# Own room for six half-row loads, four stores a row instead of eight, and no zero matmuls in a fused Fourier, mixture-of-experts and FFN kernel

## The chip, the cores and the metric

The kernel runs on one core of one Trainium2 chip. The metric is the device time of one execution in microseconds (us). TensorE (PE) does the matmuls, VectorE (DVE) and ScalarE (ACT) the elementwise work, GpSimd (POOL) part of the elementwise work and the gathers, and SyncE (SP) issues most of the DMA transfers.

## The reference

Three layers follow each other, all in float32:

```
X = rfft(x, axis=1)                                # x: 4 x 3072 x 256
Y = X @ (w_r + i w_i) + bias; Y = softshrink(Y, 0.01) on both parts
y = irfft(Y)                                       # 4*3072 tokens of 256
e = argmax(y @ w_gate); gate = softmax(...)[e]     # 8 experts, 384 places each, first come
z = gate * (relu(y_e @ w1[e]) @ w2[e])             # tokens without a place give 0
h = z @ w_in; out = (h * sigmoid(h)) @ w_out       # 256 -> 2048 -> 256
```

The 8 x 384 places are filled by the first tokens. The kernel therefore transforms the first batch and the first third of the second batch (1024 tokens), looks whether that filled all places, and leaves the rest of the second and the other two batches to a branch that does not run on these inputs.

## The kernel before, in words

The program has three stretches. First the Fourier stretch: batch 0 and the spectrum of batch 1, up to some 184 us of the profiled execution. Then experts 0 to 7: `first_ffn` (w1, relu, w2) runs for one expert after the other, and `second_ffn` (w_in, silu, w_out) for two experts together, in the order 0, 1, 2, pair 0, 3, 4, pair 1, and so on. A product in full precision is three matmuls (`mm3`, L208 to L210: high*high, low*high, high*low), so every operand is split into a high part (L192, mostly ACT) and a low part (L200, DVE or POOL).

The third stretch hides in the second: while experts 0 to 2 run, `beside` steps the generator `third(1)`, which makes the first 1024 tokens of batch 1 from the stored spectrum `b_d`, and then `route`, which gives these tokens their places. Experts 3 to 7 gather from both batches and need them. `third` works on four rows n. For each row two half rows `br` are loaded from `b_d` (L577), four matmuls make the row (L580), ACT copies it to `ao` (L585), SP stores it to `attn` (L589), and four transposes (L596) and four small matmuls (L604) give the logits. `yield 4` and `yield 5 + 2 * n` in `beside` say at which step of the expert loop a row is put into the program.

Beside these rows SP carries, in one queue and in program order: the expert weights (`st`, L1038, which ACT and then DVE or POOL split into `w`), and w_out in its 64-bit form (`nt`, L868, which DVE and ACT narrow in L874 to L881). A scheduler fixes the order of every engine's instructions when the program is built; on the chip each engine follows its own list and waits on semaphores. SP's DMAs take eight completion semaphores in turn (DMAHW0 to DMAHW7 in the rows below), so a DMA is issued only when the DMA eight places before it has landed.

`is2` does the work of `third` for all of batch 0, between 107 and 146 us. Its `turn` transposes each tile in four parts into one PSUM tile `tp` (L655) and copies it out (L657). In `experts`, `turn(xg.pop(0), 6)` brings expert 0's gathered rows into columns and adds six matmuls on zeros into a spare bank (L1079), whose result nobody reads. `pair` prepares the operands of `second_ffn` and keeps five of them in tiles of their own (`m1` to `m4`, `b2`).

Of the kernel before, what the change touches and what calls it, by code (L numbers as in the profile page):

```python
# [9 lines left out]
F32 = mybir.dt.float32  # L10
FR = mybir.dt.float32r
# [39 lines left out]
def _tables():  # L51

    n = float(S)
    t1 = np.arange(N1)
    t2 = np.arange(N2)  # L60
    c1 = np.zeros((N1, NK, 2))
    c4 = np.zeros((NK, 2, N1))
    alt = np.where(t1 % 2 == 0, 1.0, -1.0)
    c1[:, 0, 0] = 1.0
    c1[:, 0, 1] = alt
    c4[0, 0] = 1.0 / n
    c4[0, 1] = alt / n
    for k in range(1, NK):
        a = 2 * np.pi * ((k * t1) % N1) / N1
        c1[:, k, 0] = np.cos(a)  # L70
        c1[:, k, 1] = -np.sin(a)
        c4[k, 0] = 2 * np.cos(a) / n
        c4[k, 1] = -2 * np.sin(a) / n
    eye2 = np.eye(2)
    c1 = np.einsum("akr,pz->apkrz", c1, eye2).reshape(Q, Q)
    third = np.einsum("kra,pz->krpza", c4[:, :, :QB // 2], np.eye(2)).reshape(Q, QB)

    def halves(t):
        t = np.pad(t.reshape(N1, N1), ((0, 64 - N1), (0, 64 - N1)))
        return np.concatenate([t, t])  # L80

    c4 = np.concatenate([halves(c4), np.pad(third, ((0, P - Q), (0, 0)))], axis=1)
    m = np.zeros((NK, 2, N2, 2, N2))
    s = np.arange(N2)
    for k in range(1, NK):
        f = k + N1 * s
        a = 2 * np.pi * ((t2[:, None] * f[None]) % S) / S
        sg = np.where(f > S // 2, -1.0, 1.0)[None]
        co, si = np.cos(a), np.sin(a)
        m[k, 0, :, 0], m[k, 1, :, 0] = co, si  # L90
        m[k, 0, :, 1], m[k, 1, :, 1] = -si * sg, co * sg
    alt2 = np.where(t2 % 2 == 0, 1.0, -1.0)
    inv0 = np.zeros((2, N2, 2, N2))
    for half, f0 in ((0, 0), (1, N1 // 2)):
        for j in range(32):
            f = f0 + N1 * j
            if f == 0:
                continue
            a = 2 * np.pi * ((t2 * f) % S) / S
            sl = 32 * half + j  # L100
            m[0, half, :, 0, sl] = np.cos(a)
            m[0, half, :, 1, sl] = -np.sin(a)
            inv0[0, sl, half] = 2 * np.cos(a)
# [12 lines left out]
    ind[0, 0, 64] = 1.0  # L116
    ind[0, 1, 64] = 0.0
    ind = ind.transpose(1, 0, 2).reshape(2, 2 * P)
    u, q = np.arange(P) // QB, 2 * (np.arange(P) % 16) + np.arange(P) // 16 % 2
    at = TW * q + GT * u  # L120
    tri = (at[:, None] < at[None]).astype(np.float32)
    tok = 1 + at[:, None] + (TW * QB * np.arange(3)[:, None] + np.arange(GT)).reshape(1, -1)
    out = {
        "c1": c1,
        "c4": c4,
        "tab": tab,
        "inv": inv,
        "ind": ind,
        "rt": np.concatenate([tri, np.ones((P, P)), tok], axis=1),
    }  # L130
    return {k: np.ascontiguousarray(v, np.float32) for k, v in out.items()}
# [24 lines left out]
class Kernel:  # L156
# [408 lines left out]
    def third(self, b, res):  # L565
# [2 lines left out]
        v = nc.vector  # L568
        c4 = self.c4[:Q, 64:]
        bv = self.bds[b].rearrange("k (r u g) c -> (k r) u (g c)", r=4, u=4)  # L570
        od = self.attn[0][b * S:b * S + QB * TW].rearrange("(t p u g) d -> u p t (g d)", p=2, u=4, g=GT)
        res[b] = self.chosen(1)
        def rows(n):
            pt = ps.tile([P, CH], F32, tag="ps", name="ps2")
            for w in range(2):
                br = bp.tile([Q, 2, CH], F32, tag="xt", name="br", bufs=self.sb)
                nc.sync.dma_start(out=br, in_=bv[:, 2 * w:2 * w + 2, n * CH:(n + 1) * CH])  # L577
                for z in range(2):
                    u = 2 * w + z
                    ins = nc.tensor.matmul(pt[u * QB:(u + 1) * QB], c4, br[:, z], start=True, stop=True).ins  # L580
                    if b == 1 and not u:
                        self.after(ins, self.lasty)
            ao = bp.tile([P, 2, 2, P], F32, tag="ao", name="ao2")
            aof = ao.rearrange("p g h d -> p (g h d)")
            nc.scalar.copy(aof, pt)  # L585
            for u in range(4):
                for p in range(2):
                    at = u * QB + p * (QB // 2)
                    nc.sync.dma_start(out=od[u, p, :, n * CH:(n + 1) * CH], in_=aof[at:at + QB // 2])  # L589
            return ao  # L590

        def gate(n, ao):
# [27 lines left out]
    def is2(self, b, qbs, res):  # L620
# [29 lines left out]
        def turn(ao):  # L650
            aT = bp.tile([P, 2, NB, P], F32, tag="aT", name="aT")
            for h in range(2):
                tp = ps.tile([P, 4, P], F32, tag="ps", name="tp")
                for x in range(4):
                    nc.tensor.transpose(tp[:, x], ao[:, x % 2, x // 2, h * P:(h + 1) * P], self.ident)  # L655
                for ch in range(2):
                    v.tensor_copy(aT[:, h].rearrange("c b (o x t) -> c o b x t", o=2, x=4)[:, ch],  # L657
                                  tp.rearrange("c x (o b t) -> c o b x t", o=2, t=T)[:, ch, qbs[0]:qbs[0] + NB])
            return aT

        def gate(g, aT):
# [264 lines left out]
    def experts(self, again=False):  # L926
# [17 lines left out]
        def beside():  # L944

            with self.stream("b", 2, "left"):
                yield 4
                for n, _ in enumerate(self.third(1, self.res)):
                    yield 5 + 2 * n
                tiny = self.mc.tile([P, 1], F32, name="tiny")  # L950
                self.route(1, (0,), self.res)
                self.sl.extend(self.slots(self.mc, EARLY, E, self.sel, "t")[0])
                self.after(self.nc.scalar.activation(tiny, self.zt[:, 0, :1], AF.Silu).ins, self.exps)
                self.filled()
            self.po, self.mb = pool("po", **ps), pool("mb")
# [13 lines left out]
            order += [*range(q, min(q + 2, E)), E + q // 2]  # L969
        xs, self.ys, self.unit = {}, {}, {}  # L970
        xg = {e: self.gather(e) for e in order[:2]}
        xs[0] = self.turn(xg.pop(0), None if again else 6)
        ws = {e: self.weights(e, n) for e, n in zip(order[:2], (3, 4))}
        lazy = {0: (0, 1), 2: (0, 2), 3: (1, 0), 4: (0, 3), 5: (1, 1), 6: (1, 2), 7: (1, 3)}
        due = next(side, None)
# [1 line left out]
        for at, ph in enumerate(order):  # L977
# [11 lines left out]
            for m, _ in enumerate(part):  # L989
# [15 lines left out]
                if m == 5:  # L1005
                    behind = self.evicted
                if m == 6 and after < E:
                    xs[after] = self.turn(xg.pop(after), 0, behind)
            if ph < E and ph > 1 and ph % 2:
                pre = self.pair()  # L1010

# [49 lines left out]
                self.after(ins.ins, self.narrowed)  # L1061
        return xg, gw

    def turn(self, rows, zeros=0, behind=None):
        xg, gw = rows
        for j in range(SC):
            ins = self.nc.vector.tensor_scalar(xg[:, j], xg[:, j], gw[:, j:j + 1], None, ALU.mult)
            if behind:
                self.after(ins.ins, behind)
        xT = self.mx.tile([P, 2, 2, CAP], FR, tag="xT", name="xT")  # L1070
        for h in range(2):
            tp = self.ph.tile([P, CAP], F32, tag="hp", name="gtp")
            for j in range(SC):
                last = self.nc.tensor.transpose(tp[:, j * P:(j + 1) * P], xg[:, j, h * P:(h + 1) * P], self.ident)
            self.split("av", xT[:, 0, h], xT[:, 1, h], tp)
        if zeros:
            pw = self.pm.tile([P, 2 * D], F32, tag="y", name="pw")
            for n in range(zeros):
                self.after(self.nc.tensor.matmul(pw[:, :D], self.zt[:, 0, :P], self.zt[:, 0], start=True, stop=True).ins, last.ins)  # L1079
        return xT  # L1080

    def first_ffn(self, e, xT, ws):
# [26 lines left out]
    def pair(self, behind=None):  # L1109
# [6 lines left out]
        for k in range(2):  # L1116
            self.split("av", out[k][0], out[k][1], a[:, k])

        def cut(nm, src):
            t = mg.tile([P, 2, CAP], FR, name=nm, bufs=1)  # L1120
            self.split("av", t[:, 0], t[:, 1], src)
            return t[:, 0], t[:, 1]

# [2 lines left out]
        if behind:  # L1126
            self.after(ins.ins, behind)
        v.tensor_tensor(t2, b[:, 1], t1, ALU.subtract)
        m2 = cut("m2", t2)
        v.tensor_tensor(b[:, 0], b[:, 1], b[:, 0], ALU.subtract)  # L1130
        m3 = cut("m3", b[:, 0])
        m1 = cut("m1", t1)
        v.tensor_tensor(a[:, 1], a[:, 1], t2, ALU.subtract)
        m4 = cut("m4", a[:, 1])
        b2 = cut("b2", b[:, 1])
        if behind:
            self.after(self.lastact.ins, behind)
        return [*out, b2, m1, m2, m3, m4]
# [213 lines left out]
```

## Time and profile before

| | |
|---|---|
| median of three runs | 623.26 us (622.26 to 624.34) |
| the profiled execution's own time | 623.3 us |
| its span from first to last instruction | 621.5 us |
| TensorE busy with matmuls | 598.7 us (96%) |
| VectorE, ScalarE, GpSimd busy | 420.3, 338.8, 197.1 us |
| mean granted TensorE clock | 0.993 of full speed |

The profiled execution spends 1.8 us outside its span. A group of rows in the section below is one view of this execution. In the views in order of time a row gives the start in us from the span's start, the time in us, the engine, the line, the operation, output<-input, and in brackets the idle time of the engine just before it with what ended it. SPq and ACTq are the engines' own queues for DMA issues; a duration of several DMA issues with xN is from the first to the last of them.

### The profile page before, as it was taken

The page shows a single profiled execution, that of the slowest core. Times are in us where ns is not written, and L with a number is a line of the kernel's source. Part 1 is how long each engine was busy: PE and PEld are TensorE (multiplying, and loading weights), DVE is VectorE, ACT ScalarE, POOL GpSimd, SP SyncE. Part 2 cuts the span into 40 slices and gives each one's busy share as a digit, 9 for nine tenths or more (in the row PEclk, how much of TensorE's full clock was granted, in tenths as well). Part 3 has the DMA queues.
Part 4 walks back from the last instruction along what each step waited for, and adds up shares of the span by engine and source line. Part 5 has one row for each costly group of instructions (what it writes and reads, how often), then busy time and mean ns, then how long its engine had stood idle before and what let it go on. Part 6 is the DMA issues. An engine that isn't in the chain of part 4 may idle for free.

```text
span 621.5 us, 11504 instructions
## 1 busy us (share of the span) xinstructions
PE 598.7 (96%) x4128; PEld 557.0 (90%) x4128; DVE 420.3 (68%) x838; ACT 338.8 (55%) x722; POOL 197.1 (32%) x195
## 2 busy tenths in 40 slices
PE   9999999999999987989999999999999999999994
PEld 9887899668986766969999999999999999999993
DVE  2454875359967677999877687576577577485562
ACT  2535654346524545556766657556567555475561
POOL 1000110002064331456744504446403443163433
PEclk9999999999999998999999999999999999999998
DMA  8738865986266877910553533403433130010001
GB/s 207 198 98 247 293 201 153 243 245 212 69 200 196 226 191 260 310 51 26 152 183 123 155 119 112 161 26 119 145 127 110 51 126 26 13 65 26 16 2 55
DMA packets 66012, 86.09 MB, mean 139 GB/s; under 512 B 6069, under 2 KB 55865, under 8 KB 65945
## 3 DMA queue, kind: packets, MB, share of 16 engines
q1 hardware_dynamic: 53976, 69.53, 37.4%
q10 hardware_dynamic: 9664, 9.44, 5.1%
q0 software_dynamic: 2304, 6.29, 3.2%
q8 instruction: 34, 0.56, 0.4%
q14 instruction: 34, 0.27, 0.2%
HBM read 54.31 MB, written 30.93 MB: 137 GB/s over the span
## 4 chain that ended last, share of the span: by engine, by line
PE 80%; DVE 8%; issue 5%; DMA 4%; SPq 1%; ACT 1%; POOL 0%; POOLq 0%; DVEq 0%; ACTq 0%
PE o L209 7%; PE o L210 7%; PE o L208 7%; PE h L208 6%; PE h L210 6%; PE h L209 6%; PE hp L210 3%; PE hp L209 3%; PE hp L208 3%; PE y L210 3%; PE yp L208 3%; PE y L208 3%; PE y L209 3%; PE yp L210 3%; PE yp L209 3%
## 5 line engine op out<-in xcount | busy, mean ns | idle before, releaser
L1250 DVE TENSOR_TENSOR u<-h,u 128x384 f32<-128x384 f32 x224 | 117.4, 551 | 55.5 <-PE h L210 50.2
L1173 ACT ACTIVATE u<-u 128x384 f32<-128x384 f32 x128 | 64.1, 521 | 70.0 <-DVE u L1250 69.4
L209 PE MATMUL o<-wo,gl 128*128 128x256 f32 x366 | 98.1, 281 | 0.6 <-DVE gl L200 0.6
L210 PE MATMUL o<-wo,gh 128*128 128x256 f32 x366 | 98.0, 280 | 0.0
L208 PE MATMUL o<-wo,gh 128*128 128x256 f32 x366 | 86.2, 280 | 0.1
L200 POOL TENSOR_TENSOR ring<-mt,ring 128x384 fp32r<-128x384 f32 x32 | 38.2, 1195 | 131.7 <-ACT ring L192 131.6
L200 POOL TENSOR_TENSOR gl<-u,gh 128x384 fp32r<-128x384 f32 x62 | 64.9, 1065 | 30.7 <-ACT gh L192 28.2
L209 PEld LDWEIGHTS o<-wo,gl 128*128 128x128 f32 x366 | 68.8, 188 | 1.5 <-DVE gl L200 0.9
L210 PEld LDWEIGHTS o<-wo,gh 128*128 128x128 f32 x366 | 68.8, 188 | 0.0
L192 ACT CAST gh<-u 128x384 fp32r<-128x384 f32 x126 | 63.4, 510 | 5.1 <-PE o L210 3.5
L208 PEld LDWEIGHTS o<-wo,gh 128*128 128x128 f32 x366 | 64.4, 188 | 0.4 <-ACT gh L192 0.4
L208 PE MATMUL yp<-wri,xk 128*128 128x256 f32 x188 | 56.0, 298 | 0.0
L1096 ACT ACTIVATE hh<-hp 128x384 fp32r<-128x384 f32 x64 | 31.1, 490 | 43.4 <-PE hp L210 22.7
L200 POOL TENSOR_TENSOR wi<-na,wi 128x256 fp32r<-128x256 f32 (+1 forms) x8 | 8.7, 1085 | 143.7 <-ACT wi L192 143.7
L209 PE MATMUL yp<-wri,xk 128*128 128x256 f32 x188 | 53.7, 286 | 0.0
L210 PE MATMUL yp<-wri,xk 128*128 128x256 f32 x188 | 53.6, 285 | 0.0
L1097 DVE SCALAR_TENSOR_TENSOR hl<-hp,hh 128x384 fp32r<-128x384 f32 x64 | 35.0, 551 | 26.6 <-ACT hh L1096 23.1
L192 ACT CAST w<-st 128x512 fp32r<-128x512 f32 x64 | 38.8, 620 | 23.8 <-DMA st<-in_moe_w 16.0
L200 DVE TENSOR_TENSOR w<-st,w 128x512 fp32r<-128x512 f32 x53 | 36.6, 701 | 17.4 <-ACT w L192 17.2
L208 PE MATMUL y<-hh,w 128*128 128x384 f32 x128 | 44.1, 344 | 3.1 <-ACT hh L1096 3.1
L210 PE MATMUL hp<-xT,w 128*128 128x384 f32 x128 | 43.3, 339 | 0.6 <-DVE xT L200 0.6
L209 PE MATMUL hp<-xT,w 128*128 128x384 f32 x128 | 43.4, 339 | 0.4 <-DVE w L200 0.4
(254 smaller groups left out, 1541.5 us busy)
## 6 DMA issues: line engine op xcount, KB each, us to landing
st<-in_moe_w SPq DMA_DIRECT2D x64, 256.0 KB, 3.1
out<-zt SPq DMA_DIRECT2D x48, 256.0 KB, 3.1
b_d<-bo ACTq DMA_DIRECT2D x12, 512.0 KB, 3.9
mt<-mixed SPq DMA_DIRECT2D x32, 192.0 KB, 2.4
xt<-in_x SPq DMA_DIRECT2D x15, 384.0 KB, 7.2
nt<-in_moe_w_in SPq DMA_DIRECT2D x8, 512.0 KB, 4.9
nt<-in_moe_w_out SPq DMA_DIRECT2D x16, 256.0 KB, 5.0
a_d<-ao SPq DMA_DIRECT2D x8, 384.0 KB, 4.2
```

The lines of the kernel that those rows point to most:

```text
L192: self.lastact = self.nc.scalar.copy(dst, src)
L200: return e.tensor_tensor(dst, src, raw(hi), ALU.subtract).ins
L208: first = nc.tensor.matmul(out, lh, rh, start=start, stop=False)
L209: nc.tensor.matmul(out, ll, rh, start=False, stop=False)
L210: return first.ins, nc.tensor.matmul(out, lh, rl, start=False, stop=stop).ins
L1096: self.rectified = nc.scalar.activation(hh, hp, AF.Relu).ins
L1097: self.evicted = nc.vector.scalar_tensor_tensor(hl, hp, 0.0, raw(hh), ALU.max, ALU.subtract).ins
L1173: act.activation(sg, sg, AF.Silu)
L1250: v.tensor_tensor(to, h, u, ALU.add)
```

## The change

Five edits, and what the scheduler makes of them:

1. Six of the eight half rows of `third(1)` no longer wait for one another's buffer. Row 0's two take the two buffers of `xt`, as before. Rows 1 and 2 have four half rows (numbers 2 to 5 of the table `room`, two for each row), and these get room of their own: three (`bi`) in a tile that shares its place with the pair's five operands, one (`by`) in the room of `yT`, which `pair` uses later. Row 3's two take the buffers of `xt` again.
2. The columns of the table `c4` for the third are in another order (a before z instead of z before a), so that a row's 128 partitions hold the tokens in order. The row then goes out in four stores of 32 partitions instead of eight of 16. The tables of `route` follow (`q` in `_tables`), and so does `turn` in `is2`, whose transposes now write every second place of `tp`.
3. The rows enter the program at steps 7, 8, 10, 12, 14, 16 of the expert loop instead of 4, 5, 7, 9, 11, 13.
4. The six matmuls on zeros behind expert 0's transposes are gone.
5. The five operands of a pair are one tile `ms` with five parts.

```diff
@@ _tables
-    third = np.einsum("kra,pz->krpza", c4[:, :, :QB // 2], np.eye(2)).reshape(Q, QB)
+    third = np.einsum("kra,pz->krpaz", c4[:, :, :QB // 2], np.eye(2)).reshape(Q, QB)
...
-    u, q = np.arange(P) // QB, 2 * (np.arange(P) % 16) + np.arange(P) // 16 % 2
+    u, q = np.arange(P) // QB, np.arange(P) % QB
@@ third
-        od = self.attn[0][b * S:b * S + QB * TW].rearrange("(t p u g) d -> u p t (g d)", p=2, u=4, g=GT)
+        od = self.attn[0][b * S:b * S + QB * TW].rearrange("(q u g) d -> u q (g d)", u=4, g=GT)
         res[b] = self.chosen(1)
+        idle = self.mg.tile([P, 3, 2, CH], F32, tag="ms", name="bi", bufs=1)
+        room = {n + 2: idle[:Q, n] for n in range(3)}
+        room[5] = self.mh.tile([P, 2, CH], F32, tag="yT", name="by", bufs=1)[:Q]
...
-                br = bp.tile([Q, 2, CH], F32, tag="xt", name="br", bufs=self.sb)
+                br = room.get(2 * n + w)
+                if br is None:
+                    br = bp.tile([Q, 2, CH], F32, tag="xt", name="br", bufs=self.sb)
                 nc.sync.dma_start(out=br, in_=bv[:, 2 * w:2 * w + 2, n * CH:(n + 1) * CH])
...
             for u in range(4):
-                for p in range(2):
-                    at = u * QB + p * (QB // 2)
-                    nc.sync.dma_start(out=od[u, p, :, n * CH:(n + 1) * CH], in_=aof[at:at + QB // 2])
+                nc.sync.dma_start(out=od[u, :, n * CH:(n + 1) * CH], in_=aof[u * QB:(u + 1) * QB])
@@ is2, turn
-                tp = ps.tile([P, 4, P], F32, tag="ps", name="tp")
+                tp = ps.tile([P, 2, P, 2], F32, tag="ps", name="tp")
                 for x in range(4):
-                    nc.tensor.transpose(tp[:, x], ao[:, x % 2, x // 2, h * P:(h + 1) * P], self.ident)
+                    nc.tensor.transpose(tp[:, x // 2, :, x % 2], ao[:, x % 2, x // 2, h * P:(h + 1) * P], self.ident)
@@ experts
-                yield 4
+                yield 7
                 for n, _ in enumerate(self.third(1, self.res)):
-                    yield 5 + 2 * n
+                    yield 8 + 2 * n
...
-        xs[0] = self.turn(xg.pop(0), None if again else 6)
+        xs[0] = self.turn(xg.pop(0))
@@ turn
-        if zeros:
-            pw = self.pm.tile([P, 2 * D], F32, tag="y", name="pw")
-            for n in range(zeros):
-                self.after(self.nc.tensor.matmul(pw[:, :D], self.zt[:, 0, :P], self.zt[:, 0], start=True, stop=True).ins, last.ins)
@@ pair
+        ms = mg.tile([P, 5, 2, CAP], FR, tag="ms", name="ms", bufs=1)
...
-            t = mg.tile([P, 2, CAP], FR, name=nm, bufs=1)
+            t = ms[:, n]
```

The scheduler moves instructions in the stretch between the zeros and the first pair; in the part that runs, every engine's list ahead of the zeros and from the first pair's products on is as before but for names and line numbers. Three places show it. On TensorE behind expert 0's first products (`hp` is the product with w1, `y` the one with w2), before:

```order
L210 MATMUL hp<-xT,w_2170 128x384
L1079 MATMUL pw<-zt 128x256 x6
L208 MATMUL y_2155<-hh,w_2136 128x384
L209 MATMUL y_2155<-hh,w_2136 128x384
L210 MATMUL y_2155<-hl,w_2136 128x384
```

and of the change, from the same `hp` on:

```order
L210 MATMUL hp<-xT,w_2163 128x384
L208 MATMUL y_2148<-hh,w_2129 128x384
L209 MATMUL y_2148<-hh,w_2129 128x384
L210 MATMUL y_2148<-hl,w_2129 128x384
L208 MATMUL y_2149<-hh,w_2129 128x384
```

The six rows on zeros between `hp` and `y` are gone, and nothing took their place. On SP, in the first DMAs behind the spectrum (`br`, `bi` and `by` are the half rows, `bi` and `by` those with their own room; ISA rows set an address; "waits" lists the semaphores of a row), before:

```order
L577 DMA br<-b_d_1019 96x2x512 [waits DMAHW5_49,DMAHW3_49,PE_49]
L577 DMA br<-b_d_1019 96x2x512
L1038 ISA
L1038 DMA st<-in_moe_w 128x2x256 [waits DMAHW1_49,DVE_49]
L577 DMA br<-b_d_1019 96x2x512 [waits DMAHW7_49,DMAHW2_49,PE_49]
L1038 ISA
L1038 DMA st<-in_moe_w 128x2x256 [waits Pool_49]
L589 DMA attn_71<-ao_2272 16x512 [waits DMAHW4_49,Activation_49]
```

and of the change:

```order
L583 DMA br<-b_d_1019 96x2x512 [waits DMAHW5_49,DMAHW3_49,PE_49]
L583 DMA br<-b_d_1019 96x2x512
L583 DMA bi<-b_d_1019 96x2x512 [waits DMAHW1_49,PE_49]
L1042 ISA
L1042 DMA st<-in_moe_w 128x2x256 [waits DMAHW2_49,DVE_49]
L583 DMA bi<-b_d_1019 96x2x512
L583 DMA bi<-b_d_1019 96x2x512 [waits DMAHW4_49]
L583 DMA by<-b_d_1019 96x2x512
```

Six half rows now stand together, with one weight load among them and no store. Behind them come three more weight loads, four loads of w_out, a half row, the store of `mixed` and a weight load, and only then the first row's stores. Before, the third half row waited for TensorE (the buffer) and the first row's stores stood right behind it. The third place is on SP too, the second row's stores with what follows, before:

```order
L589 DMA attn_71<-ao_2337 16x512 [waits DMAHW7_49,Activation_49]
L589 DMA attn_71<-ao_2337 16x512 [waits DMAHW0_49]
L589 DMA attn_71<-ao_2337 16x512 [waits DMAHW1_49]
L589 DMA attn_71<-ao_2337 16x512 [waits DMAHW2_49]
L589 DMA attn_71<-ao_2337 16x512 [waits DMAHW3_49]
L589 DMA attn_71<-ao_2337 16x512 [waits DMAHW4_49]
L589 DMA attn_71<-ao_2337 16x512 [waits DMAHW5_49]
L589 DMA attn_71<-ao_2337 16x512 [waits DMAHW6_49]
L1038 ISA
L1038 DMA st<-in_moe_w 128x2x256 [waits DMAHW7_49,Pool_49]
```

and of the change:

```order
L593 DMA attn_71<-ao_2435 32x512 [waits DMAHW0_49,Activation_49]
L593 DMA attn_71<-ao_2435 32x512 [waits DMAHW1_49]
L593 DMA attn_71<-ao_2435 32x512 [waits DMAHW2_49]
L593 DMA attn_71<-ao_2435 32x512 [waits DMAHW3_49]
L872 DMA nt<-in_moe_w_out 128x512 [waits DMAHW4_49,DVE_49]
L872 DMA nt<-in_moe_w_out 128x512 [waits DMAHW5_49]
L872 DMA nt<-in_moe_w_out 128x512 [waits DMAHW6_49]
L872 DMA nt<-in_moe_w_out 128x512 [waits DMAHW7_49]
```

Before, the weight load behind the row waits for the row's own first store (DMAHW7 both times); with four stores the next four loads wait only for DMAs ahead of the row. ACT's list moves with it: before, its first pass over w_out (`na`, L874) comes behind expert 1's second `hh`; now the first is ahead of expert 1's first `hh`, and the second, with the first cast of `wo`, ahead of its second `hh`.

## Rows read from the trace of the kernel before

**Rows 1.** Stretch, its sum, busy us of each engine, granted clock, DMA share, GB/s.

```profile
190.00:192.50 2.50, 2.50 (x15) 2.21 (x13) 1.63 (x4) 0.81 (x2) 1.03 (x2) 1.00 0.97 338
...
240.00:244.00 4.00, 3.51 (x11) 3.52 (x12) 3.91 (x8) 2.89 (x7) 1.69 (x1) 0.57 0.81 285
...
192.50:240.50 48.00, 41.73 (x238) 31.00 (x236) 30.46 (x58) 22.16 (x46) 14.86 (x12) 1.00 0.77 215
```

**Rows 2.** TensorE in order of time, about the matmuls on zeros.

```profile
189.92 0.34 PE L210 MATMUL hp<-xT,w 128*128 128x384 f32 x1
190.09 2.75 PE L1079 MATMUL pw<-zt 128*128 128x256 f32 x12
192.50 0.52 PE L208 MATMUL y<-hh,w 128*128 128x384 f32 x1
```

**Rows 3.** GpSimd in order of time: the last low part of weights ahead of the zeros.

```profile
187.78 1.56 POOL L200 TENSOR_TENSOR w<-st,w 128x512 fp32r<-128x512 f32 x1 [1.25 <-ACT w L192]
```

**Rows 4.** TensorE in order of time, where it waits behind that.

```profile
196.76 1.05 PE L580 MATMUL ps<-br,c 96*32 96x512 f32 x4 [0.43 <-DMA br<-b_d]
198.32 1.05 PE L580 MATMUL ps<-br,c 96*32 96x512 f32 x4 [0.52 <-DMA br<-b_d]
...
224.39 0.44 PE L208 MATMUL y<-hh,w 128*128 128x384 f32 x1 [0.70 <-ACT hh L1096]
...
228.64 0.61 PE L210 MATMUL y<-hl,w 128*128 128x384 f32 x2 [1.09 <-DVE hl L1097]
...
237.43 0.66 PE L596 MATMUL tp<-ident,ao 128*128 128x128 f32 x4 [0.93 <-ACT ao L585]
240.49 0.69 PE L208 MATMUL y<-hh,w 128*128 128x384 f32 x1 [2.40 <-ACT hh L1096]
...
243.85 0.51 PE L210 MATMUL y<-hl,w 128*128 128x384 f32 x2
```

**Rows 5.** ScalarE, then VectorE in order of time: what came ahead of those waits.

```profile
223.33 0.62 ACT L192 CAST w<-st 128x512 fp32r<-128x512 f32 x1 [2.92 <-DMA st<-in_moe_w]
...
236.15 0.62 ACT L192 CAST w<-st 128x512 fp32r<-128x512 f32 x1 [4.79 <-DMA st<-in_moe_w]
...
227.24 0.88 DVE L879 TENSOR_SCALAR nsg<-nt 128x512 int32<-128x512 int32 x1 [2.10 <-DMA nt<-in_moe_w_out]
...
239.34 0.43 DVE L879 TENSOR_SCALAR nsg<-nt 128x512 int32<-128x512 int32 x1 [1.66 <-DMA nt<-in_moe_w_out]
```

**Rows 6.** SP's DMA queue in order of time, two of the four store groups.

```profile
211.72 7.41 SPq L589 DMA_DIRECT2D attn<-ao  x8
219.37 1.06 SPq L1038 DMA_DIRECT2D st<-in_moe_w  x2
...
223.61 8.98 SPq L589 DMA_DIRECT2D attn<-ao  x8
```

**Rows 7.** ScalarE in order of time: expert 1's second hh.

```profile
214.82 0.49 ACT L1096 ACTIVATE hh<-hp 128x384 fp32r<-128x384 f32 x1 [1.24 <-PE y L209]
```

**Rows 8.** DMA issues, 190 to 260 us: count, size of one, median us to landing.

```profile
st<-in_moe_w SPq DMA_DIRECT2D x20, 256.0 KB, 4.0
nt<-in_moe_w_out SPq DMA_DIRECT2D x16, 256.0 KB, 5.0
br<-b_d SPq DMA_DIRECT2D x8, 384.0 KB, 5.5
```

**Rows 9.** The chain that ended last: one load of w_out.

```profile
210.53 7.62 DMA nt<-in_moe_w_out
```

**Rows 10.** VectorE in order of time: the longest pass of the narrowing.

```profile
197.95 1.75 DVE L880 SCALAR_TENSOR_TENSOR na<-na,nsg 128x512 int32<-128x512 int32 x1
```

**Rows 11.** TensorE in order of time, transposes of batch 0 between products.

```profile
117.07 0.60 PE L655 MATMUL tp<-ident,ao 128*128 128x128 f32 x4
...
117.74 0.28 PE L208 MATMUL yp<-wri,xk 128*128 128x256 f32 x1
117.86 0.28 PE L209 MATMUL yp<-wri,xk 128*128 128x256 f32 x1
```

More of the change, by code (lines that the diff above doesn't have):

```diff
@@ L652, in turn @@
             for h in range(2):
-                tp = ps.tile([P, 4, P], F32, tag="ps", name="tp")
+                tp = ps.tile([P, 2, P, 2], F32, tag="ps", name="tp")
                 for x in range(4):
-                    nc.tensor.transpose(tp[:, x], ao[:, x % 2, x // 2, h * P:(h + 1) * P], self.ident)
+                    nc.tensor.transpose(tp[:, x // 2, :, x % 2], ao[:, x % 2, x // 2, h * P:(h + 1) * P], self.ident)
                 for ch in range(2):
-                    v.tensor_copy(aT[:, h].rearrange("c b (o x t) -> c o b x t", o=2, x=4)[:, ch],
-                                  tp.rearrange("c x (o b t) -> c o b x t", o=2, t=T)[:, ch, qbs[0]:qbs[0] + NB])
+                    v.tensor_copy(aT[:, h].rearrange("c b (o x w) -> c o b x w", o=2, x=2)[:, ch],
+                                  tp.rearrange("c x (o b t) p -> c o b x (t p)", o=2, t=T)[:, ch, qbs[0]:qbs[0] + NB])
             return aT
@@ L1007, in experts @@
                 if m == 6 and after < E:
-                    xs[after] = self.turn(xg.pop(after), 0, behind)
+                    xs[after] = self.turn(xg.pop(after), behind)
             if ph < E and ph > 1 and ph % 2:
@@ L1062, in gather, with turn @@
         return xg, gw
-    def turn(self, rows, zeros=0, behind=None):
+    def turn(self, rows, behind=None):
         xg, gw = rows
@@ L1073, in turn @@
             for j in range(SC):
-                last = self.nc.tensor.transpose(tp[:, j * P:(j + 1) * P], xg[:, j, h * P:(h + 1) * P], self.ident)
+                self.nc.tensor.transpose(tp[:, j * P:(j + 1) * P], xg[:, j, h * P:(h + 1) * P], self.ident)
             self.split("av", xT[:, 0, h], xT[:, 1, h], tp)
-        if zeros:
-            pw = self.pm.tile([P, 2 * D], F32, tag="y", name="pw")
-            for n in range(zeros):
-                self.after(self.nc.tensor.matmul(pw[:, :D], self.zt[:, 0, :P], self.zt[:, 0], start=True, stop=True).ins, last.ins)
         return xT
@@ L1117, in pair, with cut @@
             self.split("av", out[k][0], out[k][1], a[:, k])
-        def cut(nm, src):
-            t = mg.tile([P, 2, CAP], FR, name=nm, bufs=1)
+        ms = mg.tile([P, 5, 2, CAP], FR, tag="ms", name="ms", bufs=1)
+        def cut(n, src):
+            t = ms[:, n]
             self.split("av", t[:, 0], t[:, 1], src)
@@ L1128, in pair @@
         v.tensor_tensor(t2, b[:, 1], t1, ALU.subtract)
-        m2 = cut("m2", t2)
+        m2 = cut(0, t2)
         v.tensor_tensor(b[:, 0], b[:, 1], b[:, 0], ALU.subtract)
-        m3 = cut("m3", b[:, 0])
-        m1 = cut("m1", t1)
+        m3 = cut(1, b[:, 0])
+        m1 = cut(2, t1)
         v.tensor_tensor(a[:, 1], a[:, 1], t2, ALU.subtract)
-        m4 = cut("m4", a[:, 1])
-        b2 = cut("b2", b[:, 1])
+        m4 = cut(3, a[:, 1])
+        b2 = cut(4, b[:, 1])
         if behind:
```

## The prediction

> **What bounds the kernel now.** I read the table of stretches first: TensorE, its granted clock and the DMA share side by side show whether a stretch is bound by products or by something they wait for. In 190.0 to 192.5 us TensorE is busy all the time at full clock while the DMA share is 0.97; from 192.5 to 240.5 it is busy 41.73 of 48.00 us, with a DMA share of only 0.77; in 240 to 244 the granted clock is 0.57, mostly the lower of its two levels (1.2 GHz against 2.4), and VectorE is busy 3.91 of 4.00 us [rows 1]. So TensorE bounds the kernel, and some 6.3 us of idle time in the stretch that the change rewrites are to be had at most, plus what the lower clock costs.
>
> Next TensorE in order of time, where brackets name what ended each wait. The reader is to see three things. The zeros take its queue from 190.09 to 192.50, the next product has no bracket [rows 2]. Two waits of 0.43 and 0.52 us are for half rows. And four waits of 0.70, 1.09, 0.93 and 2.40 us, together 5.12, name ACT or VectorE [rows 4]. The last is followed by the lower clock: ten records from 240.49 to 243.85, 3.36 us for what takes 1.7 at 0.17 each [rows 2, 4], so some 1.6 us lost.
>
> ACT's and VectorE's own rows tell who is really late: ACT stood 2.92 us, then 4.79, for a weight load, and VectorE 2.10 and 1.66 for w_out [rows 5]. The products' `hh`, `hl` and `ao` stood behind these. SP's queue tells why the loads were late: eight stores of a row stand in it from 211.72 to 219.13, and the weight load follows at 219.37; the next eight hold it from 223.61 to 232.59 [rows 6], where the later weight load must stand behind them. A store costs about 1.0 us there, far more than its 32 KB ask for, because each is issued only when the DMA eight places before has landed.
>
> **The change part by part, against this execution (623.3 us, of which 1.8 lie outside the span; the median of the runs is 623.26, the same).**
>
> The zeros: 192.50 - 190.09 = 2.41 us less in TensorE's queue [rows 2]. The next product, `y`, needs weights whose last low part ends at 187.78 + 1.56 = 189.34 [rows 3], ahead of 190.09, so I take all of it: **-2.4**. The other bound is 0, if something later in the stretch sets the time and the products only wait longer there.
>
> The later steps: the first row's matmuls stand three steps of expert 0 later while the half rows are issued as early as before, so the two waits for them, 0.43 and 0.52 [rows 4], should go: **-1.0** (bounds -1.0 and 0; the zeros' 2.4 us bring TensorE forward, but three steps are more than that, since a step holds up to twelve products of 0.17).
>
> Own room and four stores: the order fences show two different gains. The half rows of rows 1 and 2 wait for no buffer, and the weight loads no longer stand behind eight rotating stores: with four, the loads behind them wait only for DMAs ahead of the row. 32 stores become 16 of twice the size; the bytes are the same. A group that took 7.41 or 8.98 us [rows 6] should hold the queue half as long if the count sets it, as long as before if bytes do. The share of 0.77 leaves room, 190 to 192.5 shows 338 GB/s against 215 in the stretch [rows 1], so I take it that the count does, for the most part. What it buys is the 5.12 us of waits and the 1.6 us of clock, 6.7 together: bounds 0 and -6.7. Against all of it speaks that the same bytes, and six half rows ahead of the rest, still have to come; a load of w_out took 7.62 us to land [rows 9], against 5.0 in the median [rows 8]. I take two thirds: **-4.4**.
>
> VectorE's list: with the loads earlier, the passes of the narrowing stand earlier too, ahead of some `hl`. A pass lasts 0.88 at 227.24 and up to 1.75 [rows 5, 10]. Bounds 0 and 2.5 (one long pass and a short one ahead of an `hl` that TensorE needs): **+1.5**, near the longest pass.
>
> `turn` in `is2` writes every second place of `tp`: 64 transposes, and no row of before writes so. Four of them take 0.60 us today with no wait among the products, 0.15 each for 128 columns, while products of 256 columns stand 0.12 apart [rows 11]. Streaming of the columns therefore does not set a transpose's spacing today, and at half the rate it would still fit: I take **0**. As upper bound I let each take twice its 0.15, since its 128 places lie over twice the room: 9.6 us for 64. VectorE's copy out of `tp` has as many elements and stays at its price. The shared tile `ms` and the room of `yT` cost nothing: the half rows are read by TensorE before the first pair's operands are written, and the third is done with them before it; if it were not, the pair would wait a matmul group of 1.05 us [rows 4].
>
> Sum: -2.4 - 1.0 - 4.4 + 1.5 = -6.3; 623.3 - 6.3 = **617.0 us**.
>
> **A rule against it.** The row gives `tp`'s transposes 0.15 us each with their places next to each other [rows 11]; by it the edit costs 0 and the sum stays. The Trainium skill, PSUM — Partial Sum Buffer, section Specifications (TRN2), says that PSUM is organised in lines of 8 bytes and that a pattern that is not contiguous slows a matmul significantly. No run here shows this yet; by that rule the sum would rise towards rival (c).
>
> **The rivals.**
> (a) More comes back: the narrowing hides and VectorE, busy 3.91 of 4.00 in 240 to 244 [rows 1], is relieved behind 240 as well: -2.4 - 1.0 - 6.7 = -10.1, and about 1.5 more there: 611.7. For it: every wait named hangs on loads behind stores. Against: VectorE's work is not less. Chance 0.10.
> (b) The change doesn't do what it says, since bytes and not the count of stores hold the loads: they land no earlier. -2.4 - 1.0 + 1.5 = -1.9: 621.4. For it: the share is 0.77 in the mean and 0.81 about the worst wait [rows 1]. Chance 0.16.
> (c) The places of `tp` cost their bound, -6.3 + 9.6 = +3.3: 626.6. For it speaks that TensorE has no wait there that could hide them; against it the spacing. Chance 0.06.
> (d) On the slower side as well: the six half rows crowd out w_out. ACT's list now has two passes over w_out ahead of expert 1's second `hh`. That `hh` started at 214.82 [rows 7], and would at 211.4 by the first two terms. Ahead of it SP now issues 6 x 0.384 + 4 x 0.256 + 4 x 0.256 = 4.4 MB [rows 8]. At 215 GB/s [rows 1] these take 20.5 us from 192.5, to 213.0, and a pass on VectorE, 1.75 [rows 10], still follows: the `hh` is 3.3 late, TensorE stands and the lower clock comes as it did at 240 (1.6). -2.4 - 1.0 + 3.3 + 1.6 + 1.5 = +3.0: 626.3. It decides if the rate in 192 to 213 stays under some 235 GB/s; at 338 the loads are there at 205.5. Chance 0.13.
> (e) The zeros kept the clock up: at 1.00 with them in 190 to 192.5, while behind the wait of 2.40 it was at 0.57 [rows 1, 4]. Without them the stretch falls to the lower level once: +2.4 + 1.6 on the sum, 621.0. Against: `y` follows at once, so TensorE has no gap there. The Trainium skill, TensorE: Matmul & The Clock Gate, Part 1, says that the engine is throttled by default and that activity releases it; the trace agrees at 240 us. Chance 0.05.
>
> **How the numbers follow.** The forecast holds from 613.2 (-10.1) to 619.1 (half of the 6.7, VectorE at 2.5: -2.4 - 1.0 - 3.3 + 2.5 = -4.2), chance 0.50. A measurement of this kernel tells 0.3%, or 1.9 us, from no change: faster is under 621.4, slower over 625.1. Faster: forecast, (a), (e), and half of (b): 0.73. Same: half of (b), and 0.04 for (c) or (d) at part of their price: 0.12. Slower: the rest of (c) and (d): 0.15. The range runs from (a) to the far side of (b), where VectorE costs 2.5 (622.4): 611.7 to 622.4; it leaves out (c) and (d), 0.19.
>
> **What would show it.** No row of zeros, and `y` about 0.17 behind `hp`. The half rows' waits gone from the first row's matmuls, and row 1's and 2's loads landed long before theirs. SP's groups of four stores at half the time of the groups of eight; ACT's casts without the waits of 2.92 and 4.79; the clock at 1.00 from 240 to 244. For VectorE, an `hl` behind a pass of the narrowing with TensorE waiting for it, 1 to 2 us in all. The transposes of 107 to 146 us spaced as before: if four take much over 0.60, (c) is at work. The prediction fails if ACT waits for w_out ahead of expert 1's first or second `hh` (d), or if the loads land as late as before behind fewer stores (b).

## The result, and the profile after

The changed kernel takes 615.83 us (614.16 to 617.48, 6 runs), the kernel before 622.95 us in the same comparison: a ratio of 0.9877 (0.9850 to 0.9905), some 7 us faster. The forecast was 617.0.

The profiled execution has a span of 614.9 us against 621.5, 6.65 us less. Three marks on TensorE place it: the first `y` of expert 0, the first `h` of the first pair, and the end. The first `y` stands at 192.50 before and 193.17 after, the first `h` at 261.27 and 256.13.

```
                    first y    y to first h    first h to end    span
before              192.50     68.77           360.24            621.51
change              193.17     62.96           358.73            614.86
difference          +0.67      -5.81           -1.51             -6.65
```

The change's second trace (below, under the steps) has 65.51 and 359.15 in the two middle places, so where the gain falls differs by 2.5 us between two executions of this kernel. In that one the granted clock fell once, 0.94 in 212 to 240.

The stretches of the changed kernel that answer to [rows 1]:

```profile
184.00:190.00 6.00, 5.48 (x20) 4.91 (x20) 2.11 (x5) 2.58 (x6) 2.99 (x3) 0.72 0.67 208
...
240.00:244.00 4.00, 4.00 (x29) 3.55 (x28) 3.97 (x9) 2.87 (x7) 1.81 (x2) 1.00 0.80 243
192.50:240.50 48.00, 43.60 (x266) 34.92 (x265) 41.69 (x74) 27.77 (x57) 18.36 (x15) 1.00 0.94 282
```

The stretch behind the zeros has a DMA share of 0.94 and 282 GB/s where it had 0.77 and 215. VectorE is busy 41.69 us of it instead of 30.46, so work of later stretches has come forward. In 240 to 244 the granted clock is 1.00, where it was 0.57. In 184 to 190, ahead of everything that the change touches, it is 0.72: TensorE paused there.

TensorE where the zeros stood [rows 2]:

```profile
193.00 0.33 PE L210 MATMUL hp<-xT,w 128*128 128x384 f32 x1
193.17 0.33 PE L208 MATMUL y<-hh,w 128*128 128x384 f32 x1
```

`y` follows `hp` after 0.17 us, with no wait. Its rows further on, which answer to [rows 4] (the half rows are `br`, `bi`, `by`):

```profile
201.33 0.61 PE L210 MATMUL y<-hl,w 128*128 128x384 f32 x2 [0.45 <-DVE hl L1097]
...
203.40 1.06 PE L586 MATMUL ps<-br,c 96*32 96x512 f32 x8
...
209.55 0.61 PE L208 MATMUL y<-hh,w 128*128 128x384 f32 x2 [0.65 <-ACT w L192]
...
211.86 1.06 PE L586 MATMUL ps<-bi,c 96*32 96x512 f32 x8
...
217.51 0.44 PE L208 MATMUL y<-hh,w 128*128 128x384 f32 x1 [0.70 <-ACT yf L1106]
...
218.49 0.62 PE L586 MATMUL ps<-by,c 96*32 96x512 f32 x2
...
219.13 0.60 PE L586 MATMUL ps<-bi,c 96*32 96x512 f32 x2
...
223.97 0.44 PE L208 MATMUL y<-hh,w 128*128 128x384 f32 x1 [0.48 <-ACT hh L1096]
...
225.62 0.62 PE L210 MATMUL y<-hl,w 128*128 128x384 f32 x2 [0.69 <-DVE hl L1097]
...
229.41 1.07 PE L586 MATMUL ps<-br,c 96*32 96x512 f32 x8
...
234.39 0.63 PE L608 MATMUL lg<-aT,wg 128*32 128x128 f32 x8 [0.58 <-DVE sc L557]
...
238.16 0.44 PE L208 MATMUL hp<-xT,w 128*128 128x384 f32 x1 [0.47 <-DVE xT L200]
```

Two things are to be seen. The old waits of 2.40 and 1.09 are gone and eight smaller ones stand in their place, 0.20 to 0.70, five of them on VectorE. TensorE's idle time from 192.5 to 240.5 falls from 6.27 to 4.40 us. And a row's eight records take 1.06 us together; before, each half of a row took 1.05 [rows 4], 2.1 us a row. The prediction did not look at that. In these rows "96*32" is the part of TensorE's 128 rows and 128 columns that a product fills; 32 of the columns are called a column group below.

SP's queue, beside [rows 6]:

```profile
211.00 3.72 SPq L593 DMA_DIRECT2D attn<-ao  x4
...
219.18 1.82 SPq L593 DMA_DIRECT2D attn<-ao  x4
```

These are the first two of four groups of stores. From a group's first to its last store, with other loads between them in some, the four took 4.41, 7.41, 8.98 and 5.51 us before and take 3.72, 1.82, 3.52 and 3.13 now.

### The profile page after: what moved, and what is told of

Read it like the earlier page. It is cut to its first block, busy times and chain, and to the rows that moved or that the text cites. A ratio compares the mean times of both kernels' runs of the same rounds, so it can differ in the third digit from the quotient of the medians.

```text
span 614.9 us, 11466 instructions
## 1 busy us (share of the span) xinstructions
PE 594.7 (97%) x4116; PEld 554.8 (90%) x4116; DVE 423.0 (69%) x838; ACT 338.5 (55%) x722; POOL 196.6 (32%) x195
## 5 line engine op out<-in xcount | busy, mean ns | idle before, releaser
L200 DVE TENSOR_TENSOR w<-st,w 128x512 fp32r<-128x512 f32 x53 | 38.7, 739 | 14.7 <-ACT w L192 10.8
```

The lines of the kernel that those rows point to most:

```text
L200: return e.tensor_tensor(dst, src, raw(hi), ALU.subtract).ins
```

## The experiments

Each ratio is against the kernel before on the same chip, with its 95% interval; the chip is not the same for all rows. The parts of the change are named Z (no zeros), S (four stores a row, with the new order of columns and the strided `tp`), R (own room), L (later steps); the change is Z S R L. Each run is a program of its own, and the scheduler orders its instructions anew: what a part is worth here holds the new order too.

```
parts in the kernel           ratio   interval            us from 623
Z                             0.9964  0.9951 to 0.9977    -2.2
S                             0.9926  0.9908 to 0.9945    -4.6
R                             1.0010  0.9995 to 1.0026    +0.6
L                             1.0060  1.0038 to 1.0082    +3.7
Z S                           0.9912  0.9889 to 0.9935    -5.5
Z S L                         0.9960  0.9942 to 0.9978    -2.5
Z R L                         0.9946  0.9926 to 0.9966    -3.4
Z S R                         0.9858  0.9836 to 0.9881    -8.8
Z S R, again                  0.9869  0.9840 to 0.9898    -8.2
Z S R L, the change           0.9877  0.9850 to 0.9905    -7.7
Z S R L, again                0.9888  0.9856 to 0.9919    -7.0
Z S R L, same column groups   0.9987  0.9972 to 1.0002    -0.8
Z S R, one store a row        0.9948  0.9930 to 0.9967    -3.2
```

### The zeros alone (Z)

```diff
-        xs[0] = self.turn(xg.pop(0), None if again else 6)
+        xs[0] = self.turn(xg.pop(0), None)
```

> The kernel before without the six matmuls on zeros, nothing else. Theory Z (the zeros stood in TensorE's queue ahead of products that were ready): 2.4 us less than before, 620.6. Rival W (the stretch waits for loads, which land when they land, so the waits behind grow by what the zeros gave): 622 to 623, with the waits in 224 to 241 us longer than the 5.1 us of before.

621.19 us, 2.2 less. Theory Z holds, W falls: the time did not come back as longer waits in 224 to 241. The number is a net of more than the queue, though. The four waits that the prediction listed in [rows 4] are not in this trace, and a longer one for a half row stands further ahead, with the lower clock behind it (0.91 in 192.5 to 212):

```profile
206.76 1.05 PE L580 MATMUL ps<-br,c 96*32 96x512 f32 x4 [1.94 <-DMA br<-b_d]
```

### The change without own room (Z S L)

```diff
-                br = room.get(2 * n + w)
-                if br is None:
-                    br = bp.tile([Q, 2, CH], F32, tag="xt", name="br", bufs=self.sb)
+                br = bp.tile([Q, 2, CH], F32, tag="xt", name="br", bufs=self.sb)
```

> The changed kernel with all eight half rows in the two buffers of xt again; later steps, four stores and no zeros stay. Theory G (grouping: a row's eight records run on four column groups together, 1.05 us for a row when both half rows are in, and 1.05 for each half when they come apart): rows 1 to 3 stand apart in this program's order, so 3 x 1.05 = 3.2 us more than the changed kernel, 619. Theory Q (the gain is SP's queue, where four stores no longer hold the loads): the stores are still four, so within 1 us of the changed kernel, 616 to 617.

621.13 us: more than either theory gave, 5.2 us over the change. Rows 1 to 3 come in halves; TensorE on row 2, then at the first pair:

```profile
226.09 1.05 PE L584 MATMUL ps<-br,c 96*32 96x512 f32 x4 [0.33 <-DMA br<-b_d]
...
230.70 1.05 PE L584 MATMUL ps<-br,c 96*32 96x512 f32 x4 [1.33 <-DMA br<-b_d]
...
256.35 0.42 PE L208 MATMUL h<-yT,wi 128*128 128x384 f32 x1
...
263.96 1.89 PE L762 MATMUL tb<-ft,pm 128*128 128x72 f32 x8 [4.41 <-DVE pm L750]
```

Each half takes 1.05 us, and these two wait for their loads: theory G's 3.2, and 1.7 of waits (a third wait, at 242.45, is 0.64). But the first `h` stands at 256.35, no later than in the change (256.13 and 257.57). The trace loses its time behind it, 364.65 us to the end against 358.73 and 359.15: with late halves on top of late steps the third ends so late that TensorE waits 4.41 us for `pm` of `route`, and the clock falls (0.76 in 256 to 270). So neither theory names the place where the time is lost, and how much of it the halves make and how much the steps was not told apart.

### The change with a row's halves on the same column groups

```diff
-            pt = ps.tile([P, CH], F32, tag="ps", name="ps2")
+            pts = [ps.tile([P, CH], F32, tag="ps", name="ps2") for w in range(2)]
...
-                    ins = nc.tensor.matmul(pt[u * QB:(u + 1) * QB], c4, br[:, z], start=True, stop=True).ins
+                    ins = nc.tensor.matmul(pts[w][z * QB:(z + 1) * QB], c4, br[:, z], start=True, stop=True).ins
...
-            nc.scalar.copy(aof, pt)
+            for w in range(2):
+                nc.scalar.copy(aof[2 * w * QB:2 * (w + 1) * QB], pts[w][:2 * QB])
```

> The changed kernel with the two half rows' products written to the same two column groups, in two PSUM tiles, with two copies out on ACT instead of one; loads, stores, steps and the order on SP as in the change. Theory G (grouping): a row's products take twice 1.05 us although they stand together, 4 x 1.05 = 4.2 us more than the changed kernel, 620. Theory Q (queue): TensorE's order and all loads are as in the change, so 616, plus at most 0.5 for ACT's second copy.

622.72 us, 6.9 over the change. The four rows on TensorE:

```profile
201.92 1.91 PE L586 MATMUL ps<-br,c 96*32 96x512 f32 x8
...
213.57 3.63 PE L586 MATMUL ps<-bi,c 96*32 96x512 f32 x8
...
223.07 1.03 PE L586 MATMUL ps<-bi,c 96*32 96x512 f32 x4
223.93 1.03 PE L586 MATMUL ps<-by,c 96*32 96x512 f32 x4
...
235.82 1.91 PE L586 MATMUL ps<-br,c 96*32 96x512 f32 x8
```

Eight records that stand together now take 1.91 us instead of 1.06; the row at 213.57 takes 3.63, since the granted clock was 0.50 there. So grouping is real: 0.85 a row, 3.4 in all. That fall of the clock came behind a wait of 2.08 us for an `hh` that stood on ACT behind casts waiting 3.01 us for weights; over the timed runs the mean granted clock is 0.991, against 0.995 in the change, by estimate some 2 us of the 600 that TensorE is busy. Why the weights came later with the same order of loads is open. Theory Q, alone, falls.

### The change with eight stores (Z R L), and each other part alone

```diff
-                nc.sync.dma_start(out=od[u, :, n * CH:(n + 1) * CH], in_=aof[u * QB:(u + 1) * QB])
+                for p in range(2):
+                    nc.sync.dma_start(out=od[u, p * (QB // 2):(p + 1) * (QB // 2), n * CH:(n + 1) * CH], in_=aof[...])
```

> The changed kernel with eight stores of 16 partitions a row again; own room, later steps and no zeros stay. Theory Q (queue): the weight loads stand behind eight rotating stores again, the waits of ACT and VectorE for them come back, some 2.9 us more than the changed kernel, 618.7, and store groups of 7 to 9 us. Theory G (grouping): rows still come whole, so 616 to 617.

619.62 us, 4.3 over the change: theory Q holds. ACT waits 3.18 us for a weight load at 226.41 and 3.47 for w_out at 236.37; a row's eight stores take 4.1 to 7.3 us, mostly less than the 7 to 9 expected. The stores alone are the kernel before with the diff's `_tables`, `turn` in `is2` and `od`. The one tile `ms` stays in this kernel too, as in Z S and Z S L; no run takes it by itself:

> The kernel before with the new order of columns, four stores a row and the strided tp; half rows in xt, old steps, zeros. If the parts add (A), the four stores are worth what eight cost the changed kernel, 4.3 us: 618.7. If they pay only where own room lets the loads run ahead of the rows (I): 622 to 623. If places apart in tp cost time, slower than before; the traces so far space these transposes as before, so not expected.

618.93 us, 4.6 less than before. Theory A holds, although TensorE's rows still come in halves. Room alone is the kernel before with `room`, `idle` and `ms`:

> The kernel before with own room alone (and the one tile ms that it needs); eight stores, old steps, zeros. In its order rows 1 and 2 come whole. If the parts add (A), the room is worth what the changed kernel lost without it, 5 us: 618. If grouping alone acts (G), two rows at 0.85 to 1.0: 621 to 621.5. If the stores hold the loads anyway (I, interaction): 622.5 or more.

623.91 us, no gain: case I. What tells these apart is the rate of the DMA engines in 192.5 to 240. Before:

```profile
192.50:212.00 19.50, 18.36 (x103) 13.66 (x102) 13.23 (x21) 9.28 (x19) 7.38 (x7) 1.00 0.71 209
212.00:240.00 28.00, 23.36 (x136) 17.33 (x134) 16.82 (x35) 12.38 (x27) 7.48 (x6) 1.00 0.81 216
```

The change:

```profile
192.50:212.00 19.50, 18.02 (x101) 14.71 (x103) 15.67 (x26) 10.07 (x20) 7.89 (x8) 1.00 0.98 279
212.00:240.00 28.00, 25.08 (x165) 19.96 (x161) 25.52 (x47) 17.20 (x36) 10.47 (x8) 1.00 0.93 288
```

And 212 to 240 alone, with eight stores (Z R L), with room alone (R), and with four stores alone (S), in this order:

```profile
212.00:240.00 28.00, 23.54 (x142) 18.73 (x140) 20.14 (x42) 14.75 (x31) 9.31 (x7) 0.94 0.74 225
```

```profile
212.00:240.00 28.00, 24.56 (x140) 19.28 (x138) 18.81 (x36) 15.19 (x31) 9.41 (x7) 1.00 0.76 227
```

```profile
212.00:240.00 28.00, 25.84 (x155) 20.56 (x153) 25.23 (x46) 17.00 (x36) 11.02 (x8) 1.00 0.92 279
```

With eight stores a row the rate in these rows of 212 to 240 is 216 to 227 GB/s, with four 279 to 288. In Z S, Z S L and Z S R the same row shows 266, 254 and 277, in Z and in L 235. So every kernel with four stores lies above every one with eight, and room alone changes it little. In 192.5 to 212 room counts as well: 209 before, 229 with room alone, 243 with the stores alone, 263 in Z R L.

### The steps alone (L), and the change at the old steps (Z S R)

```diff
-                yield 4
+                yield 7
                 for n, _ in enumerate(self.third(1, self.res)):
-                    yield 5 + 2 * n
+                    yield 8 + 2 * n
```

> The kernel before with the rows at steps 7, 8, 10, 12, 14, 16 alone. The prediction's step (the two waits for the first row's half rows go): 1.0 us less, 622. Rows 1 to 3 stay apart, so grouping gives nothing. Rival L (the rows' stores come later and stand ahead of later loads, the places for experts 3 to 7 later too): 623 to 625.

627.26 us, 3.7 slower: rival L, and more than its 623 to 625. The first row's two waits for half rows are gone, as the prediction has it; one of 0.99 for a half row stands at row 2 in their place:

```profile
223.56 1.05 PE L580 MATMUL ps<-br,c 96*32 96x512 f32 x4 [0.99 <-DMA br<-b_d]
```

The reverse in the changed kernel:

> The changed kernel with the rows at the old steps 4, 5, 7, 9, 11, 13; own room, four stores and no zeros stay. In its order rows 0 and 1 come with their half rows apart, rows 2 and 3 whole. Theory G (grouping, 0.85 to 1.0 us for each row that comes apart, plus the waits for half rows that come early): 2 to 3 us more than the changed kernel, 618 to 619. Rival N (the steps don't matter once the room is there): 616.

614.01 us, not slower than the change, although rows 0 and 1 do come in halves: both cases missed the sign, N by less than the intervals can tell. The pair of kernels was taken again on one chip:

> The changed kernel once more, on the same chip as the two beside it. Its first profile had a pause of TensorE at 181 to 184 us with the lower clock behind it, 2 us in all, ahead of everything that the change touches. Theory C (chance of that execution): the pause is gone, expert 0's first product starts at 183 to 185 us as in the other kernels, and the span is near 613. Theory E (an effect of the change): it is there again.

> The changed kernel with the old steps 4, 5, 7, 9, 11, 13 once more, beside the changed kernel itself. If the later steps cost time also with own room (they cost 0.6% without it): 1 to 2 us less than the changed kernel. If they are of no account there: the same within 0.3%.

616.69 and 614.96 us. The intervals overlap, the order is the same both times. The traces show where the two differ. TensorE at the first pair, the change (second trace):

```profile
257.57 0.33 PE L208 MATMUL h<-yT,wi 128*128 128x384 f32 x1
...
258.79 0.98 PE L764 MATMUL tb<-ft,pm 128*128 128x72 f32 x8
...
263.19 0.44 PE L210 MATMUL h<-ms,wi 128*128 128x384 f32 x1 [0.54 <-DVE ms L200]
...
263.65 0.34 PE L208 MATMUL h<-yT,wi 128*128 128x384 f32 x1
...
266.52 0.44 PE L208 MATMUL h<-ms,ring 128*128 128x384 f32 x1 [0.59 <-DVE u L1252]
```

and at the old steps:

```profile
254.24 0.98 PE L764 MATMUL tb<-ft,pm 128*128 128x72 f32 x8
...
257.57 0.33 PE L208 MATMUL h<-yT,wi 128*128 128x384 f32 x1
...
261.06 0.33 PE L208 MATMUL h<-yT,wi 128*128 128x384 f32 x1
```

`tb` is `route`'s last product. With later steps it stands behind the pair's first `h`: the second `h` on `yT` comes 6.08 us behind the first, with waits for VectorE, against 3.49. VectorE is as full in both, 13.83 and 13.79 of the 14.00 us from 256 to 270, but TensorE is busy 12.72 and 13.79. It was no better in the kernel before, at the old steps:

```profile
261.27 0.33 PE L208 MATMUL h<-yT,wi 128*128 128x384 f32 x1
...
263.52 0.98 PE L760 MATMUL tb<-ft,pm 128*128 128x72 f32 x8
...
268.41 0.34 PE L208 MATMUL h<-yT,wi 128*128 128x384 f32 x1
```

In the traces `tb` is ahead of the pair only where own room and the old steps come together: Z S R, R, and Z S R with one store. So beside own room the later steps take back this place of `route`; no run moves `route` alone. From the first `h` to the end the change takes 358.73 and 359.15 us, the old steps 354.94 and 355.29. They lose part of it before, since `route`'s last work then falls there: from the first `y` to the first `h` 65.09 and 65.86, against 62.96 and 65.51.

In L alone the worst wait is also `route`'s way, TensorE first, then ACT:

```profile
236.43 0.33 PE L609 MATMUL lt<-ident,ls 128*128 128x128 f32 x1 [2.97 <-ACT ls L607]
```

```profile
235.55 0.67 ACT L874 ACTIVATE na<-nt 128x512 f32<-128x512 f32 x1 [4.94 <-issue]
236.13 0.25 ACT L607 COPY ls<-lg 128x128 f32<-128x128 f32 x1
```

`ls`, a row's logits, stands on ACT behind a pass over w_out, ahead of which ACT stood 4.94 us. A wait of 2.97 on TensorE follows. This profiled execution is 1.8 us longer than that of before, 0.9 of it ahead of expert 0's first `hp`; the median is 3.7 to 4.6 longer, and the rest has no row here.

On the pause at 184 us: in the second trace of the change TensorE waits there too, 0.56 us, and the clock does not fall. Expert 0's first `hp` starts between 183.0 and 186.0 in the traces of all kernels, whatever their parts, with 186.0 the first trace of the change and 185.4 the second. Theory C for the most part; a wait also appears in Z S (0.39) and Z S R (0.49) of the same comparison and in the kernel with one store (0.95), the clock does not fall in those, and why is open.

### Two parts together (Z S), and one store a row

> The kernel before with two parts of the change, the four stores (with their order of columns and the strided tp) and no zeros; half rows in xt, old steps. If the two parts add (A): 2.2 + 4.6 us less than before, 616, as fast as the whole change, and own room and later steps together are worth nothing. If own room is needed (R): about 618 to 619, and TensorE waits for half rows br as in the kernel with four stores alone (0.41, 0.89 us).

618.03 us, 5.5 less than before: R. The half rows do hold TensorE, once for 2.00 us. Own room on top, Z S R, gives 2.7 to 3.3 us more by the ratios; one of its two intervals is clear of that of Z S, the other overlaps it.

```diff
-            for u in range(4):
-                nc.sync.dma_start(out=od[u, :, n * CH:(n + 1) * CH], in_=aof[u * QB:(u + 1) * QB])
+            nc.sync.dma_start(out=od[:, :, n * CH:(n + 1) * CH], in_=aof)
```

> The changed kernel at the old steps (614 to 615, ratio 0.986 to 0.987) with one store of 128 partitions a row instead of four. Theory C (the number of stores in the eight rotating places is what holds the loads): 12 stores fewer, at the rate of the 16 that gave 4.6 us up to 3.4 us less, 611 to 613. Rival B (with own room and four stores the loads already run ahead, what is left is VectorE and the bytes): 614 to 615, ratio 0.986 to 0.988.

619.36 us, 4.9 to 5.6 slower than four stores by the ratios: both theories fall. The number of stores alone is therefore not the price. TensorE, then ACT:

```profile
225.06 0.44 PE L208 MATMUL y<-hh,w 128*128 128x384 f32 x1 [1.68 <-ACT hh L1095]
...
234.88 0.69 PE L208 MATMUL y<-hh,w 128*128 128x384 f32 x1 [1.97 <-ACT hh L1095]
```

```profile
214.96 0.59 ACT L591 COPY ao<-ps 128x512 f32<-128x512 f32 x1 [1.89 <-DMA attn<-ao]
...
232.78 0.62 ACT L192 CAST w<-st 128x512 fp32r<-128x512 f32 x1 [2.53 <-DMA st<-in_moe_w]
```

The waits for `hh` are back, and the clock fell once behind the second. ACT's casts stand ahead of those `hh` and wait for weight loads again, one 2.53 us, and a copy to `ao` waits 1.89 for an earlier row's store, against 0.95 in Z S R. With one store the scheduler puts other loads and casts ahead of `hh`; whether that or the larger store costs more was not told apart.

## Why the prediction was right, and where not

**Right: the zeros, -2.4.** Alone they measure -2.2 (-1.4 to -3.1), and `y` stands right behind `hp`. Rival (e) is refuted: no gap, and the clock behind `y` is 1.00. Where the clock does fall in Z alone, TensorE had waited 1.94 us for a half row just before. That the rest moves too was not in this term: in that trace `y` to the first `h` is 2.0 us shorter than before and the rest behind it 1.0 longer. So the queue's 2.4 is there (expert 0's first `hp` to its first `y` takes 7.11 against 9.49 us), but that the total comes so near to it is partly luck.

**Wrong: "the later steps: -1.0".** The two waits for half rows did go [rows 4], but the step priced only them. It named nothing of what the third feeds: `route` ends later too, and with own room its last work then stays in the first pair, as it did before the change, where the old steps bring it ahead. Alone the steps cost 3.7 us (2.4 to 5.1). In the whole change they cost 1.1 to 1.2 by the ratios, with overlapping intervals.

**Own room and four stores, -4.4: too small, with gains that were not in its reasons.** With VectorE's +1.5 the forecast for them is -2.9; on top of the zeros (Z S R against Z) they give 5.9 to 6.6. The four stores alone give 4.6, with the mechanism given: the rate of the loads rises from 216 to 279 GB/s. That refutes rival (b). Of rival (d) the sign came and the price did not. ACT waits for w_out ahead of expert 1's first and second `hh`, which the prediction named as a way to fail:

```profile
213.03 0.68 ACT L878 ACTIVATE na<-nt 128x512 f32<-128x512 f32 x1 [1.40 <-DMA nt<-in_moe_w_out]
...
215.40 0.69 ACT L878 ACTIVATE na<-nt 128x512 f32<-128x512 f32 x1 [1.31 <-DMA nt<-in_moe_w_out]
```

The second `hh` starts at 217.34, later than the 214.82 of before, but the rate in 192.5 to 212 is 279, over the 235 under which (d) would decide, and TensorE waits 0.70 there with the clock at 1.00. Own room was counted for its waits; alone it is worth nothing, and on top of the stores some 3 us. Part is a term that the prediction lacks: four of a row's eight records run together with the other four if both half rows are in. From first to last record the rows' matmuls took 8.4 us before, with 1.1 of waits for half rows besides, and take 4.4 after, without one. Another part, at the old steps, is `route` ending ahead of the pair. The price of 1.05 for a group stood in [rows 4], with "96*32" beside it; that four such products fill the 128 columns was to be read there.

**VectorE, +1.5: near in size, as far as the waits tell.** The waits for `hl` in the rows above are 0.45 and 0.69, and one at 202.85 is 0.20; 1.3 in all. Those for `sc` and `xT` add 1.05. No run takes this term alone.

**`tp`, 0: right.** The transposes of the change, as [rows 11]:

```profile
118.06 0.60 PE L659 MATMUL tp<-ident,ao 128*128 128x128 f32 x4
```

Four take 0.60 us as before, and two in succession stand 0.109 us apart in both kernels (the prediction's 0.15 is the 0.60 shared among four). The Trainium skill, PSUM — Partial Sum Buffer, section Specifications (TRN2), says that a pattern that is not contiguous slows a matmul significantly; for transposes of 128 columns of float32 at a stride of two this trace does not agree. Rival (c) is refuted.

**The sum.** -6.3 forecast, -6.65 between the profiled executions. The parts are not the same: -2.4 for the zeros, +3.0 ahead of the first `hp` (1.0 from the first 7 us of the program, 2.0 with the pause), -5.8 to the first pair, where the forecast's other terms make -3.9 (-1.0 - 4.4 + 1.5), and -1.5 behind it, where it had nothing and only rival (a) had 1.5. In the second trace the last two are -3.3 and -1.1. The pause stands in these rows:

```profile
184.52 2.07 PE L490 MATMUL bp<-cl,c 128*128 128x256 f32 x4 [1.05 <-ACT bo L192]
186.03 0.88 PE L208 MATMUL hp<-xT,w 128*128 128x384 f32 x1
```

So the total was met partly because a chance loss ahead stood against a gain that was not foreseen. By the ratios, taken over many executions, the change gives 7.0 to 7.7, a little more than forecast.

**The parts don't add.** Z and S alone make 6.8, together 5.5. R is worth 0 beside eight stores and 3 beside four. Taking the stores or the room out of the change costs 4.3 and 5.2, with the zeros' 2.2 far more than the 7.7 of the whole. In R alone `route` does end ahead of the pair, and from the first `h` to the end it takes 3.9 us less than before; but from `y` to the first `h` it takes 4.1 more, with the rate at 227 and VectorE busy 16.00 of the 16.00 us from 240 to 256. That late loads cause this is argued, not shown. And own room is what makes the later steps bearable: L costs 3.7 alone, 3.0 on top of Z S, and some 1 on top of Z S R.

## What to carry to other kernels

Where DMAs rotate through a few completion places, count the places that small stores take and read the DMA rate of the stretch: a low rate with waits for loads was here a queue, and not bytes. Fewer is not always better: one store a row kept the rate (268) and lost the time. Before a producer is moved later, follow all it feeds, to the place where its last work falls; the wait that it saves was the smaller part here. And the best version here keeps the old steps: Z S R, at 0.9858 and 0.9869, beats the kernel before clearly and the change in both comparisons, by less than the intervals can tell.

## What the runs showed of the hardware that was not expected

- Matmuls that fill 32 columns each run side by side: four started 7 ns apart and took together what two take, 1.06 us for a row of eight records against 1.05 for half a row. On the same two column groups the row takes 1.91.
- A float32 transpose that writes every second place of PSUM costs as much here as one that writes them in a row, 0.60 us for four.
- Four stores of 64 KB in place of eight of 32 KB raised the DMA rate of a whole stretch of 28 us from 216 to 279 GB/s, with the same bytes to move; one of 256 KB gave 268 and no time.
